# A two-layer MLP kernel: product 7 of matmul 2 in block 0 by an inner Strassen level

## The chip, the cores and the metric

The kernel runs on one core of a Trainium2 chip. The core has a matmul engine (TensorE, "PE" in the profile, with its weight loads shown as "PEld"), three elementwise engines (VectorE "DVE", ScalarE "ACT", GpSimd "POOL"), an engine that mainly issues transfers (SyncE "SP"), 16 DMA engines, a working memory of 128 partitions (SBUF) and eight accumulator banks of 512 fp32 values per partition (PSUM). Each engine runs its own instruction list in order; lists are tied together by semaphores. The metric is device time in microseconds; lower is better.

## The reference

```python
def reference(x, w1, b1, w2, b2):
    y = _layernorm(x, axis=-1)
    h = _gelu(jnp.einsum("bsd,df->bsf", y, w1) + b1)
    return jnp.einsum("bsf,fd->bsd", h, w2) + b2
```

x is 1 x 2048 x 1024, w1 is 1024 x 3584, w2 is 3584 x 1024, all in bf16. _layernorm subtracts the mean over the last axis and divides by the square root of the variance plus 1e-5; _gelu is the tanh approximation. The work is two matmuls of 2048 x 1024 x 3584 with a normalisation ahead, a gelu between and a bias at each.

## The kernel before, in words

**Blocks and products.** The 2048 tokens are two blocks of 1024 (s = 0 and 1). Within a block each of the two matmuls is done by Strassen's method in Winograd's form: operands are cut into quarters, seven products of quarters replace eight, and sums of quarters are formed before and after. For matmul 2 the left quarters are h[11], h[12], h[21], h[22] (512 tokens x 14 slices of 128 features), their sums S1 to S4, and the right quarters B11 to B22 of w2 with their sums T1 to T4. The order of products is SEQ2 = 1, 5, 2, 6, 7, 3, 4. Product 6 multiplies S2 by T2, product 7 multiplies S3 by T3. The sum of products 1 and 6 is called U here: it enters the output quarters 12 (with products 5 and 3), 21 (with 7 and 4) and 22 (with 7 and 5).

**Plain and inner products.** A product can be plain or inner. A plain one (plain, L974) is four groups, one per 128 tokens, of 14 matmuls with 512 columns each (L978). An inner one (inner, L1036) applies Strassen again: seven sub-products of 14 matmuls with 256 columns (sub, L1060, matmuls at L1063), after four sums of the left operand (tt, recorded at L854), and sums of the right one (inner_sums, L998: one large sum at L1022, or two where split is set, and two more at L854). inner_sums of block 0 also stores the sums to DRAM (keep), and block 1 loads them from there. An inner product's results leave PSUM in six VectorE adds and two ScalarE copies (k1, k5, k2, o11, o22, o12, o21, and a seed copy, all recorded at L942 and L962), each sub-product after the third waiting for an earlier one. INNER says which products are inner:

```python
INNER = ((1, 5, 2, 3, 4), SEQ2)
```

that is five of seven in block 0 and all of block 1. Since block 1 needs inner sums of T2 and T3 that block 0 does not make, t_inner (L1361) makes them during matmul 1 of block 1: it loads T2 or T3 to x_sb, forms three sums on VectorE (L1370) and stores them.

**Buffers.** yw_sb holds the normalised, transposed input during matmul 1 and pieces of w2 during matmul 2; w2a_sb holds two quarters of w2 (slots A and B); w1_sb, t1_sb, h_sb and o_sb are reused for sums once their first content is used up. sn_sb is 12 slots of fp32 rows for partial results. x_sb holds the eight input tiles of the next block, normalised by ScalarE (ln_act2, L464) during matmul 2 of block 0 and transposed into yw_sb by DMA (dma_T, L517). A tile of the second half has to wait with one of its transposes for the end of product 2, whose weights lie where it goes.

**Around the change.** In block 0 product 6 accumulates on U's banks hb, seeded with product 1's result. O12 (L1323) adds product 5 and keeps the result for output quarter 12. Product 7 then accumulates in the same four banks (L1329); four VectorE adds (L1336) make output quarter 22, and four ScalarE copies, O3 (L1340), keep the banks for product 4, which makes quarter 21.

**Order.** A planner (Planner.place, L149) places every operation when the kernel is built: it keeps a time for each engine, adds an estimated cost for each operation, and picks on the engine that is free first the one with the lowest due time among those that can start. ORDER adds a hand-made offset to the due time of some 170 operations by name. The outcome is a fixed list for each engine, with waits where an operation needs another engine's result or a freed buffer.

Of the kernel before, what the change touches and what calls it, by code (L numbers as in the profile page):

```python
# [32 lines left out]
INNER = ((1, 5, 2, 3, 4), SEQ2)  # L33
# [6 lines left out]
    G1_5g_0_5:5.5 G1_5g_1_5:8.8 G2_5g_0_3:-15.8 G2_5g_1_3:0.8 G3_5g_0_3:7.3 G3_5g_0_5:-4.7 G3_5g_1_1:-25.3  # L40
    G4_5g_1_1:13 G6_5g_0_5:-21 G7_5g_0_3:9.2 G7_5g_0_5:6.5 M11_1:8.3 M15_0:17 M24_0:-3.1 M27_1:5.7 M43_0:-8.5
    M47_0:7.7 M51_1:7.2 M57_0:16.8 M6_0_0:3.3 M72_1:-20.2 O12_0_1:11.2 O12_0_3:8.4 P1_0_6:10.3 P1_0_9:-1.1
    P1_1_2:-2.7 P1_1_3:-18.7 P1_1_6:0.2 P2_0_12:-1 P2_0_5:0.7 P3_0_10:-9.9 P3_0_11:5.1 P3_0_12:-7.3 P3_0_2:-10.3
    P3_1_6:9.8 P4_0_3:7.4 P4_0_9:-17.7 P4_1_0:40.5 P4_1_1:54.4 P4_1_3:2 P6_0_12:-3.6 P6_0_4:1.1 P6_1_11:4.1
    P7_0_6:-33.7 c7_0_11:2.3 c7_0_5:1.2 c7_0_8:-5.5 c7_0_9:8.4 c7_1_12:9.1 c7_1_13:1.2 g12_1_1:13.1 g12_1_3:2.2
    g21_1_8:25.8 g22_0_2:1.3 g22_0_3:1.6 gS0_5g_1_3:20 gS1_5g_0_3:-6.6 gS1_5g_0_5:11.2 gS3_5g_0_5:14.9 g_0_3_2:-14.6
    hS2_0_1:-7.5 hS3_1_0:8.3 hS4_0_1:-4.8 hS4_0_3:39 iS3_1_1_0:41 iS3_2_0_0:8.3 iS5_3_1_0:28.6 iS5_4_0_0:-14.1
    iS5_5_0_0:-10 iS6_5_0_0:-3.7 iT4_1_0_0:4.1 iT4_2_0_0:3.8 iT4_3_0_0:13.3 iT5_3_0_0:14.2 iT6_1_0_0:4.6
    iT6_2_0_0:1.3 iT6_4_0_0:6.6 iT6_5_0_0:-8.9 k5_3_1:16.7 k5_5g_0_5:35.6 o12_3_0:-17 pT1_2:-34.8 pT1_3:15 pT1_6:4.8
    pT2_1:1.7 pT2_2:7.7 pT3_3:10.8 pT3_5:-2.2 pT4_0:-7.2 pT4_3:-4.3 pT4_4:-7 pT4_5:-2.4 pT4_6:7.9 plain_0_7_2None:35  # L50
    plain_0_7_3None:8.5 pw2_0:-4.4 r11_5g_1_5:-18.2 r12_5_0:10.8 r22_1_0:14.3 r22_5g_0_3:33.7 s2_2_0:-7.2
    sd1_0_2:11.5 sn1_0_9:12.1 sn1_1_10:2.8 sn1_1_5:-0.5 sn5_0_4:-29.1 st0_5_0:-3.9 w1T13_1_0:3.4 w1T1_0_4:30.1
    w1T1_0_6:-5.1 w1T1_1_2:3.5 w1T2_1_1:26.1 w1T3_0_6:-17.7 w1T4_1_3:15 w1_0_0_1:9.9 w1_0_3_0:-7.9 w1_0_5_0:-24
    w1_0_5_1:-0.6 w1_1_0_0:0.7 w1_1_6_1:-1.9 w6_0_11:-4.1 w6_0_5:-9.5 w6_1_5:-44.2 wi5_3:20.8 x0_0_1:-11.2 x1_0:4.8
    y1_6:-8.5 yS1_1_0:6.2 yS2_0_0:8.2 yS2_1_0:-3.4 yS4_1_0:8.6 yi13_1:14.5 yi2_0:-15 yt0_6_0:-2.3
# [5 lines left out]
LAT = 0.12  # L61
PE_LAT = 0.2
# [43 lines left out]
class Planner:  # L106
# [42 lines left out]
    def place(self):  # L149
# [12 lines left out]
        while left:  # L162
# [35 lines left out]
            free[e] = r + c  # L198
# [60 lines left out]
def bass_standalone__mixer_channel_mlp__prompt_kernel(  # L259
# [24 lines left out]
    with ExitStack() as es:  # L284
# [584 lines left out]
        x_gate = {}  # L869
        PU = 2  # L870
# [58 lines left out]
        def mm2_block(s, W):  # L929
# [10 lines left out]
            last_ = {}  # L940
            done = lambda p: users[p]
# [10 lines left out]
            def bank_q(h_):  # L952
                return ps[:, h_.k, :].rearrange("p (v c) -> p v c", v=2)
# [82 lines left out]
            def inner(p, a, Yo, xb, war, O=None, bias=None, out=None, gate=(), ogate=(), kk=None, tmp=None, tail=False):  # L1036
# [21 lines left out]
                subs, ev = {}, {}  # L1058

# [68 lines left out]
                k1 = copy(kk_q, lambda: bank_q(c0), (subs[1], *gate), end(1), f"k1_{nm}", alloc=hk or tmp)  # L1128
# [55 lines left out]
            def last_block():  # L1184
# [82 lines left out]
                give(hold[7], sub7)  # L1267
                for i in range(2):
                    ho = Holder(outs, 2)
                    q = 10 * i + 11  # L1270
                    rows = lambda g, i=i: sn_sb[:, g.k + 2 * i:g.k + 2 * i + 2, :].rearrange(
                        "p j (v c) -> p v j c", v=2)
                    f = [add("DVE", 1.22, lambda e, i=i, ho=ho, rows=rows: plus(
                        e, o_sb[:, ho.k:ho.k + 2, :].rearrange("p v (j c) -> p v j c", j=2), rows(gw), rows(g5)),
                        (okq[q], okq[q + 1], *O12.values()), pt[7] + 7 * SUB + 0.1 * i, f"o22_{s}_{i}", alloc=ho,
                        frees=(g5,) if i else ())]
                    store(22, 2 * i, 2, ho, f, pt[7] + 7 * SUB)
# [5 lines left out]
            def war_of(subs, p=None):  # L1283
                return {(c, r): [subs[r]] + ([ti_st[p][r]] if c == "T" and r in ti_st.get(p, {}) else [])
                        for c in "ST" for r in subs}
# [41 lines left out]
            B[4] = load_w2(s, "H", "T4", done(6) + flat(S3, S4), pt[1] + 0.1, late=3.0)  # L1327

            M7 = plain(7, S3, B[7], hb, False, [(o,) for o in O12])  # L1329
            w1_use[n - 2] = w1_use[n - 2] + [M7[1]]  # L1330
            g3 = Holder(snaps, 4)
            O3 = []
            for t in range(TH):
                ho = Holder(outs)
                at = pt[7] + (t + 1) * SLOT2
                f = dve(lambda e, t=t, ho=ho: plus(e, o_sb[:, ho.k, :].rearrange("p (j c) -> p j c", j=2), bank_t(hb[t]),  # L1336
                                                   tile_of(g5, t)), (M7[t], *ok_t[t // 2]), at, f"o22_{s}_{t}", alloc=ho,
                        frees=(g5,) if t == TH - 1 else ())
                store(22, t, 1, ho, (f,), at)
                O3.append(copy(lambda t=t: tile_of(g3, t), lambda t=t: bank_t(hb[t]), (f, *O3[:1]), at + 0.7, f"O3_{s}_{t}",  # L1340
                               alloc=g3 if t == 0 else None, frees=(hb[t],)))

            sub3 = inner(3, S4, inner_sums(3, B[3], Y0, war_of(sub2, 2), True), X0, war_of(sub2), O=(g12, {11: O12[1], 12: O12[1], 21: O12[3], 22: O12[3]}), out=12)
            for m in (n - 1, n):
                w1_use[m] = w1_use[m] + done(3) + kept[3]
            for m in (n - 1, n):
                for k in range(1, 5):
# [5 lines left out]
                  halves(h_flat[21]), war4, O=(g3, {11: O3[1], 12: O3[1], 21: O3[3], 22: O3[3]}), out=21)  # L1353
# [3 lines left out]
            return {"A": done(3), "B": done(4) + kept[4], "C": done(2), "ring": ring, "p5": done(5), "p2": done(2), "outs": stores}  # L1357
# [49 lines left out]
        for s in range(NSB):  # L1407
# [27 lines left out]
            if s == 0:  # L1435
                W = {5: t1q, 1: t11, "C": last}
            else:
                x_end = [o for i in range(NT) for o in x_free[(s, i)]] + wfree["outs"]
                e6 = t_inner(6, 1, x_end + w1_use[NC], base1[s] + 0.2 * T_MM1)
                e7 = t_inner(7, 2, e6 + w1_use[NC + 2], base1[s] + 0.45 * T_MM1)  # L1440
                W = {"A": wfree["A"], "B": wfree["B"], "x": e7, "C": last}
            wfree = wf = mm2_block(s, W)
            if s + 1 < NSB:
                for c in range(N_W1):
                    load_w1(s + 1, c, base2[s] + 40 + c)
                for i in range(NT):
                    if i not in LN_EARLY:
                        load_x(s + 1, i, [*x_gate[i]], base2[s] - 4 + i)
                        k = (0, 1, 2, 2, 3, 4)[i]
                        ln_act2(s + 1, i, base2[s] + 6 + 8 * k,  # L1450
                                wf["ring"] + ([], [], wf["p5"], wf["p5"], wf["p2"])[k])
                    dma_T(s + 1, i, base2[s] + 20 + 6.3 * i, ((*last, *(wf["C"] if i >= TH else ())), last))
                y_sums(s + 1, base1[s + 1] - 4, wf["C"])
# [59 lines left out]
```

## Time and profile before

| | us |
|---|---|
| median of 9 runs (lowest, highest) | 338.63 (338.17, 340.62) |
| the profiled execution, its own time | 338.17 |
| its span, first to last instruction | 336.4 |
| TensorE busy in the span | 329.5 |
| VectorE busy | 281.7 |
| ScalarE busy | 173.4 |
| GpSimd busy | 22.3 |

The profile is that of one execution. Its span leaves out what lies around the instructions, so it is shorter than the execution's own time. L12 means line 12 of the kernel; where several operations go through one helper they share its line, so that L942 is any VectorE add made by dve, L962 any ScalarE copy made by copy and L854 any sum made by sums. A row of a group gives the output and inputs, partitions x elements and type, the count, the busy time, the mean duration in nanoseconds and the idle time of that engine just before. Consecutive instructions of one engine can overlap by a little at their ends. Block 0's matmul 1 ends and its matmul 2 begins near 95 us of the span; matmul 1 of block 1 begins near 172, its matmul 2 near 257.

### The profile page before, as it was taken

The page shows a single profiled execution, that of the slowest core. Times are in us where ns is not written, and L with a number is a line of the kernel's source. Part 1 is how long each engine was busy: PE and PEld are TensorE (multiplying, and loading weights), DVE is VectorE, ACT ScalarE, POOL GpSimd, SP SyncE. Part 2 cuts the span into 40 slices and gives each one's busy share as a digit, 9 for nine tenths or more (in the row PEclk, how much of TensorE's full clock was granted, in tenths as well). Part 3 has the DMA queues.
Part 4 walks back from the last instruction along what each step waited for, and adds up shares of the span by engine and source line. Part 5 has one row for each costly group of instructions (what it writes and reads, how often), then busy time and mean ns, then how long its engine had stood idle before and what let it go on. Part 6 is the DMA issues. An engine that isn't in the chain of part 4 may idle for free.

```text
span 336.4 us, 6035 instructions
## 1 busy us (share of the span) xinstructions
PE 329.5 (98%) x2399; PEld 223.5 (66%) x2399; DVE 281.7 (84%) x381; ACT 173.4 (52%) x292; POOL 22.3 (7%) x47
## 2 busy tenths in 40 slices
PE   4999999999999999999999999999999999999996
PEld 4977445455468885547875555544545888888885
DVE  3996789998999999979999878886738879999984
ACT  5775978566786687612113666765676521010200
POOL 2320120000020413200000000000000000000000
PEclk9899999999999999999999999999999999999999
DMA  7796999797869999899859549739971999998103
GB/s 237 265 205 185 356 348 323 245 330 257 286 238 301 364 355 337 223 308 384 323 171 331 172 181 337 286 136 287 350 233 54 383 314 361 338 364 278 64 0 127
DMA packets 80310, 89.47 MB, mean 266 GB/s; under 512 B 15130, under 2 KB 67226, under 8 KB 79770
## 3 DMA queue, kind: packets, MB, share of 16 engines
q1 hardware_dynamic: 80138, 88.95, 81.4%
q8 instruction: 19, 0.31, 0.4%
q10 hardware_dynamic: 144, 0.13, 0.1%
q14 instruction: 9, 0.07, 0.1%
HBM read 61.81 MB, written 24.38 MB: 256 GB/s over the span
## 4 chain that ended last, share of the span: by engine, by line
PE 93%; ACT 3%; POOL 1%; DVE 1%; DMA 1%; issue 0%
PE ps L767 42%; PE ps L1063 34%; PE ps L978 7%; PE ps L619 5%; PE ps L692 5%; DMA x_sb<-in_x_dram 1%; POOL st_sb L488 1%; PE ps L504 1%; ACT t_sb L474 1%; ACT t_sb L469 1%; PE ps L1068 0%; ACT sn_sb L962 0%; ACT ps L962 0%; DVE st_sb L418 0%; ACT x_sb L491 0%
## 5 line engine op out<-in xcount | busy, mean ns | idle before, releaser
L767 PE MATMUL ps<-yw_sb,t_sb 128*128 128x512 f16 x336 | 80.0, 379 | 0.0
L767 PE MATMUL ps<-yw_sb,w_sb 128*128 128x512 f16 x312 | 74.7, 379 | 0.0
L792 ACT ACTIVATE h_sb<-ps,b_sb 128x512 f16<-128x512 f32 x78 | 52.9, 687 | 37.0 <-PE ps L767 32.3
L767 PEld LDWEIGHTS ps<-yw_sb,t_sb 128*128 128x128 f16 x336 | 32.8, 98 | 35.9 <-DVE ps L807 0.6
L767 PEld LDWEIGHTS ps<-yw_sb,w_sb 128*128 128x128 bf16 x312 | 30.3, 98 | 33.1 <-ACT ps L780 0.3
L854 DVE TENSOR_TENSOR h_sb<-h_sb 128x2048 f16<-128x2048 f16 (+2 forms) x36 | 38.6, 1085 | 7.3 <-ACT h_sb L792 5.3
L962 ACT COPY sn_sb<-ps 128x512 f32<-128x512 f32 x27 | 15.5, 583 | 32.9 <-DVE o_sb L942 18.2
L1063 PE MATMUL ps<-w2a_sb,h_sb 128*128 128x256 f16 (+1 forms) x252 | 30.3, 273 | 0.0
L942 DVE TENSOR_TENSOR sn_sb<-ps,sn_sb 128x512 f32<-128x512 f32 x35 | 24.0, 688 | 5.3 <-PE ps L1063 4.5
L1063 PEld LDWEIGHTS ps<-w2a_sb,h_sb 128*128 128x128 f16 x252 | 24.7, 98 | 3.9
L942 DVE TENSOR_TENSOR o_sb<-ps,sn_sb 128x512 bf16<-128x512 f32 (+1 forms) x29 | 19.3, 670 | 6.3 <-PE ps L1063 3.7
L978 PE MATMUL ps<-w2a_sb,h_sb 128*128 128x512 f16 x112 | 24.5, 379 | 0.0
L1063 PE MATMUL ps<-w_sb,t_sb 128*128 128x256 f16 x196 | 23.4, 273 | 0.1
L962 ACT COPY ps<-sn_sb 128x512 f32<-128x512 f32 x12 | 7.1, 589 | 30.3 <-PE ps L1063 24.6
L780 ACT COPY ps<-ps 128x512 f32<-128x512 f32 x26 | 14.9, 577 | 14.5 <-PE ps L767 14.5
L587 DVE TENSOR_TENSOR t_sb<-w_sb,t_sb 128x1024 f16<-128x1024 bf16 x26 | 17.9, 688 | 3.6 <-DMA w_sb<-in_w_dram 2.4
L1063 PEld LDWEIGHTS ps<-w_sb,t_sb 128*128 128x128 f16 x196 | 19.0, 98 | 2.7 <-ACT sn_sb L962 0.4
L792 ACT ACTIVATE h_sb<-sn_sb,b_sb 128x512 f16<-128x512 f32 x26 | 18.5, 716 | 3.8 <-DVE sn_sb L821 2.9
L807 DVE TENSOR_TENSOR ps<-ps,sn_sb 128x512 f32<-128x512 f32 x26 | 17.6, 694 | 3.3 <-PE ps L767 3.1
L978 PEld LDWEIGHTS ps<-w2a_sb,h_sb 128*128 128x128 f16 x112 | 10.9, 98 | 12.8
L821 DVE TENSOR_TENSOR sn_sb<-ps,sn_sb 128x512 f32<-128x512 f32 x20 | 13.6, 687 | 4.5 <-PE ps L767 4.4
L619 PE MATMUL ps<-yw_sb,w_sb 128*128 128x128 f16 x256 | 16.9, 227 | 0.4 <-DVE yw_sb L511 0.4
(125 smaller groups left out, 485.6 us busy)
## 6 DMA issues: line engine op xcount, KB each, us to landing
w_sb<-in_w_dram SPq DMA_DIRECT2D x28, 512.0 KB, 5.8
x_sb<-in_w_dram SPq DMA_DIRECT2D x21, 256.0 KB, 6.0
w_sums<-x_sb SPq DMA_DIRECT2D x21, 256.0 KB, 3.8
w2a_sb<-w_inner_sums SPq DMA_DIRECT2D x12, 448.0 KB, 7.3
x_sb<-in_x_dram SPq DMA_DIRECT2D x15, 256.0 KB, 6.1
w_inner_sums<-w_sb SPq DMA_DIRECT2D x4, 896.0 KB, 8.3
x_sb<-w_sums SPq DMA_DIRECT2D x2, 1792.0 KB, 9.1
w_sb<-w_inner_sums SPq DMA_DIRECT2D x8, 448.0 KB, 7.0
```

The lines of the kernel that those rows point to most:

```text
L587: return add("DVE", 0.65, lambda e: e.tensor_tensor(out=tv(k), in0=x0, in1=x1, op=ALU.subtract), [*deps, *war.get(k, ())], prio + 0.5 * k, ...
L619: fn = [(lambda e, b=b, hb=hold[f], f=f, k=k, t=t: e.matmul(ps[:, hb.k, t * P:(t + 1) * P], lhsT=lhs[:, k, f * P:(f + 1) * P], rhs=yop[f"A ...
L692: fn = [(lambda e, k=k, v=v: e.matmul(ps[:, bank[r].k, v * QN:(v + 1) * QN], lhsT=xo()[:, k, v * P:(v + 1) * P], rhs=yv()[:, k, :], start= ...
L767: fn = [(lambda e, k=k: e.matmul(ps[:, hold[p].k, :], lhsT=lhs[:, k, :], rhs=yop[yo][:, k, :], start=(first and k == 0), stop=(k == KH - 1 ...
L780: return e.copy(out=dst, in_=src) if o_.eng == "ACT" else e.tensor_copy(dst, src)
L792: r = h_ok[(s, q, u)] = add("ACT", 0.70, lambda e: e.activation(out=dst, in_=src(), func=ACT.Gelu_apprx_tanh, bias=b1_sb[:, f:f + 1], scal ...
L807: o2 = add("DVE", 0.7, lambda e: e.tensor_tensor(out=b5v(b5), in0=b5v(b0), in1=v5(), op=ALU.add), (P6, *o5), pt[7] - SLOT, f"w6_{nm}", all ...
L854: o = add("DVE", cost2(w * dst.shape[-1]), lambda e, k0=k0, k1=k1: e.tensor_tensor(out=dst[:, k0:k1, :], in0=a[0][:, k0:k1, :], in1=b[0][: ...
L942: plus = lambda e, out, x, y: e.tensor_tensor(out=out, in0=x, in1=y, op=ALU.add)
L962: return act(lambda e: e.copy(out=out(), in_=src()), deps, at - 5, name, **k)
L978: fn = [(lambda e, k=k, t=t: e.matmul(ps[:, banks_[t].k, :], lhsT=a[0][:, k, t * P:(t + 1) * P], rhs=b[0][:, k, :], start=(first and k == ...
L1063: fn = [(lambda e, k=k, j=j: e.matmul(ps[:, bank[r].k, j * HI:(j + 1) * HI], lhsT=x[0][:, k, j * P:(j + 1) * P], rhs=y[0][:, k, :], start= ...
```

## The change

Product 7 of matmul 2 in block 0 becomes an inner product. Its weights' sums are formed in block 0 and stored; t_inner is no longer called for product 7. U is copied from the banks to gu by four ScalarE copies ahead of it, each bank freed by O12, which now follows the copy. The inner product adds its results onto gu, and two VectorE adds of twice the size make output quarter 22 from gu and product 5. Product 4 adds onto gu as well. The place for k1, product 7's first copy, is row 4 of x_sb, and so that copy waits until tile 4 of block 1 has been transposed (x_late); later loads into x_sb wait for k1's readers (x_users). Product 3's sums now wait for product 7's sub-products and stores, where they waited for product 2's. The planner takes 0.08 us off each VectorE and 0.09 us off each ScalarE operation for the overlap with the next, and ORDER has new entries throughout.

```diff
-INNER = ((1, 5, 2, 3, 4), SEQ2)
+INNER = ((1, 5, 2, 7, 3, 4), SEQ2)
 ...
+OVL = {"DVE": 0.08, "ACT": 0.09}
 ...
-            free[e] = r + c
+            free[e] = r + c - OVL.get(e, 0.0)
 ...
+        x_late = []
 ...
+                s_read[id(subs)] = {5: s2[1][0], 6: s4[1][0]}
 ...
-                k1 = copy(kk_q, lambda: bank_q(c0), (subs[1], *gate), end(1), f"k1_{nm}", alloc=hk or tmp)
+                first_k[p] = k1 = copy(kk_q, lambda: bank_q(c0), (subs[1], *gate), end(1), f"k1_{nm}", alloc=hk or tmp)
 ...
-
-            M7 = plain(7, S3, B[7], hb, False, [(o,) for o in O12])
-            w1_use[n - 2] = w1_use[n - 2] + [M7[1]]
-            g3 = Holder(snaps, 4)
-            O3 = []
+            gu = Holder(snaps, 4)
+            U = []
             for t in range(TH):
-                ho = Holder(outs)
-                at = pt[7] + (t + 1) * SLOT2
-                f = dve(lambda e, t=t, ho=ho: plus(e, o_sb[:, ho.k, :].rearrange("p (j c) -> p j c", j=2), bank_t(hb[t]),
-                                                   tile_of(g5, t)), (M7[t], *ok_t[t // 2]), at, f"o22_{s}_{t}", alloc=ho,
-                        frees=(g5,) if t == TH - 1 else ())
-                store(22, t, 1, ho, (f,), at)
-                O3.append(copy(lambda t=t: tile_of(g3, t), lambda t=t: bank_t(hb[t]), (f, *O3[:1]), at + 0.7, f"O3_{s}_{t}",
-                               alloc=g3 if t == 0 else None, frees=(hb[t],)))
-
-            sub3 = inner(3, S4, inner_sums(3, B[3], Y0, war_of(sub2, 2), True), X0, war_of(sub2), O=(g12, {11: O12[1], 12: O12[1], 21: O12[3], 22: O12[3]}), out=12)
+                U.append(copy(lambda t=t: tile_of(gu, t), lambda t=t: bank_t(hb[t]), (M6[t], *U[-1:]),
+                              pt[6] + (t + 1) * SLOT2, f"U_{s}_{t}", alloc=gu if t == 0 else None))
+                O12[t].frees = (hb[t],)
+                O12[t].deps.append(U[-1])
+
+            gw, okq, sub7 = inner(7, S3, inner_sums(7, B[7], Y0, war_of(sub2, 2)), X0, war_of(sub2),
+                                  O=(gu, {11: U[1], 12: U[1], 21: U[3], 22: U[3]}), kk=x_sb[:, TH, :].bitcast(F32))
+            x_late.append((first_k[7], (TH,)))
+            w1_use[n - 2] = w1_use[n - 2] + [sub7[5]]
+            f = []
+            for i in range(2):
+                ho = Holder(outs, 2)
+                q = 10 * i + 11
+                rows = lambda g, i=i: sn_sb[:, g.k + 2 * i:g.k + 2 * i + 2, :].rearrange("p j (v c) -> p v j c", v=2)
+                f = [add("DVE", 1.22, lambda e, i=i, ho=ho, rows=rows: plus(
+                    e, o_sb[:, ho.k:ho.k + 2, :].rearrange("p v (j c) -> p v j c", j=2), rows(gw), rows(g5)),
+                    (okq[q], okq[q + 1], *O12, *f), pt[7] + 7 * SUB + 0.1 * i, f"o22_{s}_{i}", alloc=ho,
+                    frees=(g5,) if i else ())]
+                store(22, 2 * i, 2, ho, f, pt[7] + 7 * SUB)
+            x_users = [okq[11]]
+
+            sub3 = inner(3, S4, inner_sums(3, B[3], Y0, war_of(sub7, 7), True), X0, war_of(sub7), O=(g12, {11: O12[1], 12: O12[1], 21: O12[3], 22: O12[3]}), out=12)
 ...
             inner(4, A[22], inner_sums(4, B[4], [two(w2b), *halves(w2b)[2:]], war4),
-                  halves(h_flat[21]), war4, O=(g3, {11: O3[1], 12: O3[1], 21: O3[3], 22: O3[3]}), out=21)
+                  halves(h_flat[21]), war4, O=(gw, okq), out=21, gate=(f[-1],))
 ...
-            return {"A": done(3), "B": done(4) + kept[4], "C": done(2), "ring": ring, "p5": done(5), "p2": done(2), "outs": stores}
+            return {"A": done(3), "B": done(4) + kept[4], "C": done(2), "ring": ring, "p5": done(5), "p2": done(2), "outs": stores + x_users}
 ...
-                e6 = t_inner(6, 1, x_end + w1_use[NC], base1[s] + 0.2 * T_MM1)
-                e7 = t_inner(7, 2, e6 + w1_use[NC + 2], base1[s] + 0.45 * T_MM1)
-                W = {"A": wfree["A"], "B": wfree["B"], "x": e7, "C": last}
+                e6 = t_inner(6, 1, x_end + w1_use[NC], base1[s] + 0.25 * T_MM1)
+                W = {"A": wfree["A"], "B": wfree["B"], "x": e6, "C": last}
 ...
+                for o, tiles in x_late:
+                    o.deps += [d for i in tiles for d in x_free[(s + 1, i)]]
```

## The prediction, made before the result was known

> **What bounds the kernel now.** I read the page's first part, then the waits of TensorE, then TensorE's timeline across matmul 2 of block 0, then VectorE's.
>
> From the page, busy time of each engine:
>
> ```profile
> PE 329.5 (98%) x2399; PEld 223.5 (66%) x2399; DVE 281.7 (84%) x381; ACT 173.4 (52%) x292; POOL 22.3 (7%) x47
> ```
>
> All that TensorE waited for (total us, times, longest):
>
> ```profile
> PE ps L504 <- DVE x_sb L429: 2.8, 1, 2.8
> PE ps L400 <- POOL ones L375: 1.0, 1, 1.0
> PE ps L619 <- DVE yw_sb L511: 0.4, 1, 0.4
> ```
>
> All three lie in the head. From then on TensorE is never seen waiting, so the end is set by the sum of its matmuls. Any matmul time removed is gained, provided nothing makes it wait.
>
> TensorE's timeline around product 7 (start, us):
>
> ```profile
> 126.71 6.21 PE L978 MATMUL ps<-w2a_sb,h_sb 128*128 128x512 f16 x28
> 132.75 1.69 PE L1063 MATMUL ps<-w_sb,h_sb 128*128 128x256 f16 x14
> 134.28 1.69 PE L1063 MATMUL ps<-yw_sb,t_sb 128*128 128x256 bf16 x14
> 135.81 18.29 PE L978 MATMUL ps<-w2a_sb,h_sb 128*128 128x512 f16 x84
> 153.94 1.69 PE L1063 MATMUL ps<-w2a_sb,h_sb 128*128 128x256 bf16 x14
> 155.47 1.69 PE L1063 MATMUL ps<-w_sb,t_sb 128*128 128x256 f16 x14
> ```
>
> A 512-column matmul costs (132.75 - 126.71) / 28 = 0.2157 us. An inner group of 14 with 256 columns costs 155.47 - 153.94 = 1.53 us, or 0.109 each. The 84 matmuls are the rest of product 6 (28) and all of product 7 (56), so product 7 starts near 141.9.
>
> The second engine to read is VectorE, by stretches (length, then PE, PEld, DVE, ACT, POOL busy; clock; DMA share; GB/s):
>
> ```profile
> 60.00:75.00 15.00, 15.00 (x75) 7.25 (x74) 14.65 (x25) 8.96 (x15) 0.00 (x0) 1.00 0.84 281
> 95.20:178.80 83.60, 83.48 (x630) 61.27 (x629) 77.33 (x87) 39.23 (x67) 11.91 (x18) 1.00 0.92 301
> 178.80:195.00 16.20, 16.20 (x89) 8.51 (x87) 13.68 (x24) 10.05 (x17) 0.00 (x0) 1.00 0.78 265
> ```
>
> From 95.2 to 178.8, the whole of matmul 2 in block 0, VectorE is busy 77.33 of 83.6 us. It is idle for 6.3, and DMA is busy for 92%. VectorE sets nothing yet, but it has hardly any room.
>
> **What the Trainium skill says.** "TensorE: Matmul & The Clock Gate", section Back-to-back issue gap, gives N/2.4 + 2.5 ns: 215.8 and 109.2 for 512 and 256 columns. The trace agrees (215.7, 109). "VectorE: DVE Perf Modes", section The perf-mode tier table, says that adding two tensors runs at one element a cycle when one is in PSUM, and at two for 16-bit SBUF data; the rows agree (512 f32 from PSUM 688 ns, 1792 f16 1085 ns). "Perfetto Trace Analysis", section Optimizing Scalar/DVE Operations, says that the write acknowledgement of one instruction overlaps the next. The trace agrees: adds of 0.68 us start 0.60 apart, 1.08 ones 1.00 apart, 1.22 ones 1.13 apart. I therefore count 0.08 less than the row's duration each. The same section advises giving work to ScalarE when VectorE is full, which the U copies do.
>
> **The change part by part.**
>
> TensorE: out go 56 x 0.2157 = 12.08 us. In come 7 groups x 14 x 0.109 = 98 x 0.109 = 10.68. Gain 1.40 us. The weight loads rise from 56 to 98, but run beside the matmuls in the inner groups already.
>
> VectorE in block 0. Removed: four adds into the output, 4 x 0.60 = 2.4. Added, all by periods: the sums of T3's quarters 1.93 + 1.0 + 1.0 = 3.9; the four sums of S3's quarters 4 x 1.0 = 4.0; six evictions of the inner product 6 x 0.60 = 3.6; two final adds over 1024 fp32 elements, 2 x 1.14 = 2.3, from this row of block 1:
>
> ```profile
> L942 DVE TENSOR_TENSOR o_sb<-sn_sb 128x1024 bf16<-128x1024 f32 x2 | 2.5, 1225 | 0.1
> ```
>
> Net +11.4 us between about 127 and 165. In block 1 the preparation of product 7's weights disappears (three sums at 222.7 to 226.9, 3.9 us, one load of 1792 KB and three stores of as much), but TensorE didn't wait for them, so they pay nothing. Those stores now leave in block 0.
>
> ScalarE: U's four copies replace those of product 7's result (0.58 us each). The inner product adds two. Its 39.2 busy of 83.6 us hide them; uncovered they would be 1.2 us.
>
> SyncE: three stores of sums come in, two of four output stores go, and the transposes and loads behind them slip by about half a microsecond of issue each.
>
> Now the fit. TensorE would reach the end of block 0 1.4 us earlier with 11.4 us more VectorE work before it, so VectorE must find 12.8 us by the first matmuls of block 1 that need its sums (t_sb at 178.79). It can find:
> - its idle time, 6.3, and 0.08 at each of some 12 gaps that would close, 1.0: together 7.3. Not all: the fullest stretch shown, 60 to 75, reaches 98%, so 2% of 83.6 = 1.7 stays idle. 5.6.
> - work done ahead of need. These lines lie before 178.79:
>
> ```profile
> 169.57 1.22 DVE L543 TENSOR_TENSOR yw_sb<-yw_sb 128x2048 f16<-128x2048 f16 x1
> 171.56 1.22 DVE L543 TENSOR_TENSOR yw_sb<-yw_sb 128x2048 f16<-128x2048 f16 x1
> 173.89 1.22 DVE L543 TENSOR_TENSOR yw_sb<-yw_sb 128x2048 f16<-128x2048 f16 x1
> 177.59 1.42 DVE L587 TENSOR_TENSOR t_sb<-w_sb,t_sb 128x1024 f16<-128x1024 bf16 x2
> ```
>
> Two of the y sums (2.3), the two weight sums (1.2) and one output add (0.6) can come later: 4.1. Then 178.8 to 195, now 84% busy, has to carry them.
> - matmuls of block 1 that need no sum. Those of two units already lie at 172 to 177. One more of 0.86 us may find a bank and its weights.
>
> Together 10.6, leaving 2.2 us that TensorE waits.
>
> Tile 4 and DMA: the copy k1 of product 7 goes into x_sb's row 4 and waits for both transposes of that tile. One of them can't start before product 2 ends at 135.8, and the last now leave late:
>
> ```profile
> 143.56 3.68 SPq L520 DMA_TRANSPOSE yw_sb<-x_sb  x2
> ```
>
> k1 must start by 144.2 (two groups into product 7, less its own 0.6). A transpose lands a median 5.3 us after issue, so 135.8 + 1.5 + 5.3 = 142.6 is in time if it goes first. Behind k1 on ScalarE stand the seed of the next product and normalisation of tile 5; product 7's third group waits for k1. B22, issued at 142.3, also meets 1.8 MB more stores, some 6 us at 300 GB/s, with product 3's second sum needing it by about 152. Bound for both: nothing (covered by product 6 and by 3 us between B22's landing and use) to 3 us. I take 0.6, as queues are 92% full.
>
> The remade table and the planner's overlap of 0.08/0.09 move other instructions. The gain can't exceed TensorE's total idle, 336.4 - 329.5 = 6.9, nearly all head and tail; the loss is open. I take 0, bounds -0.3 and +2.
>
> Sum: -1.4 + 2.2 + 0.6 = +1.4. The profiled execution took 338.17 us, 1.8 around its span of 336.4, so its successor would take about 339.6; the median of the runs is 0.5 higher, 338.63, giving **340.0 us**.
>
> **Rivals.**
> - All is hidden: idle time is used to the end (7.3), early work moves (4.1), two to three free matmul groups fill in (1.7 to 2.6). That is at least 13.1 against 12.8, so TensorE keeps its 1.4 us: 337.2. For: no waits now, ScalarE half idle, early transposes movable. Against: 84 us without one gap on an in-order engine. It decides if VectorE's share in this stretch passes 99%.
> - Even: part of the idle time gained, TensorE waits 0.4 to 2.4 us: about 338.6. For: the lower bound and my estimate stand only 2 us apart.
> - A transfer becomes the bound: tile 4's transpose or B22 arrives 3 us late on top of VectorE's 2.2: -1.4 + 2.2 + 3 = +3.8, 342.4. For: DMA share above 1.0 in the stretches from 145 to 160. Against: SyncE's order was written anew.
> - The change does not do what it says: the inner groups might run slower than 1.53 us. Products 2 and 3 show the same form at that rate; I give it nothing.
>
> **Numbers.** Chances: VectorE short, 339.65 to 341.5, 0.33; all hidden 0.25; even 0.30; transfer 0.12. Faster and slower begin at 0.3%, 1.0 us, about what a measurement of this kernel can tell from no change: 0.25 faster, 0.30 same, 0.45 slower. The likeliest case's own range is 339.6 to 341.5. The range of all, 337.0 to 342.6, takes in the hidden case and the transfer's centre.
>
> **What would show it.** Right: 98 L1063 matmuls in place of 56 L978 ones, the groups 1.53 us apart; VectorE 97% or more busy from 127 to 180; TensorE waiting for VectorE's sums or evictions in products 7, 3, 4 and the first unit of block 1, 2 to 3 us in all; the L543 sums later than 172. Wrong: no TensorE waits there (then 337.2), gaps on VectorE while TensorE waits for DMA or for k1 (then the transfer), or new waits far from block 0's matmul 2, which would be the table's.

## The result and the profile after

The changed kernel takes 342.77 us (median of 10 runs, 341.38 to 344.96) where the kernel before takes 338.73 in the same measurement (32 runs, 337.87 to 340.62): the ratio is 1.0123, 95% interval 1.0106 to 1.0140. It is slower by 4.0 us. The profiled execution took 342.23 us, its span 340.5, so it too stands 4.06 above that of before. (A correction to the description above: the table ORDER of the kernel before has 134 entries, not some 170.)

Busy time of each engine, from the page of the changed kernel:

```profile
PE 330.4 (97%) x2441; PEld 227.5 (67%) x2441; DVE 286.0 (84%) x389; ACT 173.8 (51%) x294; POOL 27.0 (8%) x47
```

There are 42 more matmuls, as there should be. GpSimd has the same 47 instructions, yet they take 4.7 us longer; nothing in the change gives GpSimd other work, and this is the first hint.

What TensorE waited for (total us, times, longest; the three rows left out lie in the head):

```profile
PE ps L1070 <- ACT ps L968: 1.8, 1, 1.8
...
PE ps L1070 <- DVE sn_sb L948: 0.9, 2, 0.6
...
PE ps L770 <- DVE t_sb L590: 0.4, 1, 0.4
PE ps L1070 <- DVE w_sb L857: 0.2, 1, 0.2
```

Before, nothing stood here outside the head. The longest of the new waits is not for VectorE but for a copy of ScalarE. TensorE's timeline through product 7 shows where it is:

```profile
142.65 1.69 PE L1070 MATMUL ps<-w2a_sb,h_sb 128*128 128x256 f16 x14
144.18 1.69 PE L1070 MATMUL ps<-w_sb,t_sb 128*128 128x256 f16 x14
147.68 1.70 PE L1070 MATMUL ps<-w2a_sb,h_sb 128*128 128x256 f16 x14 [1.81 <-ACT ps L968]
149.21 1.69 PE L1070 MATMUL ps<-w_sb,t_sb 128*128 128x256 f16 x14
151.17 1.70 PE L1070 MATMUL ps<-w2a_sb,t_sb 128*128 128x256 f16 x14 [0.26 <-DVE sn_sb L948]
153.50 1.70 PE L1070 MATMUL ps<-w_sb,t_sb 128*128 128x256 f16 x14 [0.63 <-DVE sn_sb L948]
```

Two groups start 1.53 us apart, as predicted; the third comes 3.50 after the second. Below I count a gap as the distance from one matmul's start to the next, less 0.2157 us for 512 columns or 0.109 for 256. Counted so, the first gap is 1.97 us, where the profile's own count of idle time is 1.81. In the profile of the changed kernel the gaps between 127 and 185 us are 1.97, 0.43, 0.79 and 0.13 in product 7, 0.40 at 170.8, and 0.17 and 0.57 at 182.6 and 183.6: together 4.46. Before, they are 0.0.

ScalarE's timeline at the same place:

```profile
134.07 1.24 ACT L494 ACTIVATE x_sb<-x_sb,st_sb,rstd_sb 128x1024 f16<-128x1024 bf16 x1 [3.68 <-POOL st_sb L491]
...
143.51 1.24 ACT L494 ACTIVATE x_sb<-x_sb,st_sb,rstd_sb 128x1024 f16<-128x1024 bf16 x1 [1.84 <-POOL st_sb L491]
144.66 2.47 ACT L968 COPY sn_sb<-ps 128x512 f32<-128x512 f32 x4
147.02 0.60 ACT L968 COPY ps<-sn_sb 128x512 f32<-128x512 f32 x1
147.54 0.59 ACT L968 COPY x_sb<-ps 128x512 f32<-128x512 f32 x1
```

L494 is the normalisation of a tile of block 1 (its result is called y): first tile 2's, then tile 5's. Behind tile 5's y stand the four copies of U, the seed and k1. TensorE had finished product 6 at 142.65, so U's last bank was ready when ScalarE still waited for GpSimd: the copies came 2 us late, and with them the seed (the copy ps<-sn_sb at 147.02), for which the third group of product 7 waits.

The kernel before has the same y, and there too it waited for GpSimd:

```profile
140.98 1.24 ACT L491 ACTIVATE x_sb<-x_sb,st_sb,rstd_sb 128x1024 f16<-128x1024 bf16 x1 [2.18 <-POOL st_sb L488]
```

It ended at 142.22, 0.4 us after product 6 (141.85), and the first copy behind it started at 145.80, when VectorE's add had released it. In the changed kernel it ended at 144.75, 2.1 us after product 6, with U's copies behind it. The wait was thus there to be seen ahead of the change; that it would end later was not.

VectorE shows the same wait from its side. Its first line is three of hS3's sums in one row (S3, the left operand of product 7); the last two are two of O12's four adds, which need U's copies:

```profile
131.04 2.95 DVE L857 TENSOR_TENSOR h_sb<-h_sb 128x2048 f16<-128x2048 f16 x3
...
145.32 0.69 DVE L948 TENSOR_TENSOR sn_sb<-ps,sn_sb 128x512 f32<-128x512 f32 x1 [2.81 <-ACT sn_sb L968]
146.49 0.69 DVE L948 TENSOR_TENSOR sn_sb<-ps,sn_sb 128x512 f32<-128x512 f32 x1 [0.47 <-ACT sn_sb L968]
```

VectorE loses 3.28 us just ahead of the stretch in which it has no spare time: from 147 to 180 us it is busy 32.76 of 33.0. GpSimd's timeline says why ScalarE waited. Each tile has three instructions of 128x1 elements; the first two lines are the second and third for tile 2, the last is the third for tile 5:

```profile
129.28 1.65 POOL L488 TENSOR_TENSOR rstd_sb<-vpe_sb,nhalf 128x1 f32<-128x1 f32 x1
131.00 3.03 POOL L491 TENSOR_TENSOR st_sb<-mv_sb,rstd_sb 128x1 f32<-128x1 f32 x1
...
143.28 0.19 POOL L491 TENSOR_TENSOR st_sb<-mv_sb,rstd_sb 128x1 f32<-128x1 f32 x1
```

The same instruction takes 0.19 us and 3.03 us. The long one runs from 131.00 to 134.03, just as long as VectorE's sums from 131.04 to 133.99. Tile 2's three took 5.0 us together (129.00 to 134.03); in the kernel before they took 1.35 (128.61 to 129.96):

```profile
129.15 0.55 POOL L485 TENSOR_TENSOR rstd_sb<-vpe_sb,nhalf 128x1 f32<-128x1 f32 x1
129.77 0.19 POOL L488 TENSOR_TENSOR st_sb<-mv_sb,rstd_sb 128x1 f32<-128x1 f32 x1
```

Beside these two VectorE ran additions from PSUM. The tiles are normalised one after another, so part of tile 2's delay is still in tile 5's y. SyncE's list, too, stands behind that y. Its issues in the changed kernel:

```profile
140.33 5.64 SPq L523 DMA_TRANSPOSE yw_sb<-x_sb  x4
146.02 0.58 SPq L353 DMA_DIRECT2D w_inner_sums<-w_sb  x1
146.64 1.99 SPq L523 DMA_TRANSPOSE yw_sb<-x_sb  x1
148.68 1.43 SPq L353 DMA_DIRECT2D w2a_sb<-in_w_dram  x2
```

Tile 5's transposes wait for its y, and B22 (w2a_sb) is issued behind them at 148.68; before, it was issued at 142.33, ahead of the last two transposes.

The profile thus adds up: -1.40 (less matmul time) + 4.46 (gaps) + 0.88 (the head: the last of its 128-column matmuls starts at 31.66, before at 30.78) = 3.94 of the 4.06 us. The head's share need not be the change's work: that start moves by as much among kernels with the same head (last section).

### The profile page after: what moved, and what is told of

The parts are those of the page before. It is cut to its first block, busy times and chain, and to the rows that moved or that the text cites. A ratio compares the mean times of both kernels' runs of the same rounds, so it can differ in the third digit from the quotient of the medians.

```text
span 340.5 us, 6132 instructions
## 1 busy us (share of the span) xinstructions
PE 330.4 (97%) x2441; PEld 227.5 (67%) x2441; DVE 286.0 (84%) x389; ACT 173.8 (51%) x294; POOL 27.0 (8%) x47
## 5 line engine op out<-in xcount | busy, mean ns | idle before, releaser
L770 PE MATMUL ps<-yw_sb,w_sb 128*128 128x512 f16 x312 | 75.5, 379 | 0.0
L770 PEld LDWEIGHTS ps<-yw_sb,w_sb 128*128 128x128 bf16 x312 | 30.3, 98 | 31.7 <-ACT ps L783 0.6
L1070 PE MATMUL ps<-w2a_sb,h_sb 128*128 128x256 f16 (+1 forms) x280 | 33.5, 273 | 1.8 <-ACT ps L968 1.8
L948 DVE TENSOR_TENSOR sn_sb<-ps,sn_sb 128x512 f32<-128x512 f32 x40 | 27.1, 686 | 8.0 <-PE ps L1070 4.6
L1070 PEld LDWEIGHTS ps<-w2a_sb,h_sb 128*128 128x128 f16 x280 | 27.1, 98 | 6.1 <-ACT ps L968 2.1
L1070 PE MATMUL ps<-w_sb,t_sb 128*128 128x256 f16 x238 | 28.3, 273 | 0.7 <-DVE sn_sb L948 0.6
L1070 PEld LDWEIGHTS ps<-w_sb,t_sb 128*128 128x128 f16 x238 | 23.1, 98 | 4.5 <-DVE sn_sb L948 0.9
L948 DVE TENSOR_TENSOR o_sb<-ps,sn_sb 128x512 bf16<-128x512 f32 (+1 forms) x25 | 16.7, 667 | 5.3 <-PE ps L1070 3.2
L857 DVE TENSOR_TENSOR t_sb<-h_sb 128x1792 f16<-128x1792 f16 x16 | 17.4, 1086 | 1.6 <-ACT h_sb L795 0.8
L622 PEld LDWEIGHTS ps<-yw_sb,w_sb 128*128 128x128 bf16 x256 | 16.1, 104 | 2.0 <-DMA w_sb<-in_w_dram 1.3
L1070 PE MATMUL ps<-w_sb,h_sb 128*128 128x256 f16 (+1 forms) x126 | 15.2, 273 | 0.2 <-DVE w_sb L857 0.2
```

What stands on the lines that cost most here:

```text
L622: fn = [(lambda e, b=b, hb=hold[f], f=f, k=k, t=t: e.matmul(ps[:, hb.k, t * P:(t + 1) * P], lhsT=lhs[:, k, f * P:(f + 1) * P], rhs=yop[f"A ...
L770: fn = [(lambda e, k=k: e.matmul(ps[:, hold[p].k, :], lhsT=lhs[:, k, :], rhs=yop[yo][:, k, :], start=(first and k == 0), stop=(k == KH - 1 ...
L857: o = add("DVE", cost2(w * dst.shape[-1]), lambda e, k0=k0, k1=k1: e.tensor_tensor(out=dst[:, k0:k1, :], in0=a[0][:, k0:k1, :], in1=b[0][: ...
L948: plus = lambda e, out, x, y: e.tensor_tensor(out=out, in0=x, in1=y, op=ALU.add)
L1070: fn = [(lambda e, k=k, j=j: e.matmul(ps[:, bank[r].k, j * HI:(j + 1) * HI], lhsT=x[0][:, k, j * P:(j + 1) * P], rhs=y[0][:, k, :], start= ...
```

## The experiments

All start from the changed kernel. Most move entries in the finished lists, after the planner, with this helper, and change nothing else:

```diff
+        def move(e, names, ahead_of):
+            mv = [o for n in names for o in order[e] if o.name == n]
+            rest = [o for o in order[e] if o not in mv]
+            k = next(k for k, o in enumerate(rest) if o.name == ahead_of)
+            order[e] = rest[:k] + mv + rest[k:]
```

### e1_u_first: ScalarE's list alone

```diff
+        move("ACT", [f"U_0_{t}" for t in range(TH)], "y1_5")
```

> Edit: the changed kernel, with the four copies of U moved ahead of tile 5's last normalisation step in ScalarE's list; nothing else moves. Queue theory (U stands behind a step that waits for GpSimd, and this makes both TensorE's first gap and VectorE's idle time, which is then missing later): TensorE's gap of 1.97 us at 145.6 shrinks below 0.5, VectorE's idle time of 3.3 us ahead of O12 below 1, and 2 to 3.5 us come back, so 339.3 to 340.8. Shortage theory (VectorE has too much work and the sum of the gaps is fixed by it): the first gap goes, but the later ones grow by as much; less than 1 us comes back, 341.8 to 342.8.

345.53 us (342.65 to 347.26, 4 runs), 1.018 times before (1.0111 to 1.0249): above both forecasts. The gap behind U is gone, and one wait of the sort shown above has taken its place:

```profile
PE ps L1070 <- DMA w2a_sb<-in_w_dram: 3.5, 1, 3.5
```

That is B22, issued at 152.01 behind tile 5's transposes, needed at 154.8. So two queues, not one, stand behind tile 5's y, and the first delay had hidden the second. The median is not this edit's price alone: the profiled execution (347.26) also lost 2.24 us between 115 and 123 us (see e8_y_behind), and 1.5 us in a stretch at half the granted clock that begins 0.9 us after this wait (last section).

### e2_u_b22_first: both queues

```diff
+        move("ACT", [f"U_0_{t}" for t in range(TH)], "y1_5")
+        move("SP", ["is7_0", "w2_0_B22_0", "w2_0_B22_1"], "yt1_5_0")
```

> Edit: as e1_u_first, and in SyncE's list the first store of product 7's sums and the two loads of B22 move ahead of tile 5's two transposes, so that they don't wait for tile 5 either. Queue theory: B22 is asked for at about 143 instead of 148.7; if e1_u_first shows TensorE or VectorE waiting for B22 at product 3 (1 to 3 us near 152), that wait goes here and the time is 338.5 to 340; if it shows none, the time is that of e1_u_first within 0.5. Shortage theory: no change against e1_u_first.

340.87 us (13 runs), ratio 1.0066 (1.0037 to 1.0095): about half of the loss is back, less than the queue theory said. Neither U nor B22 shows a gap any more. Part of what is left is the next thing on SyncE behind the same transposes: block 1's first weights, issued at 152.05, make TensorE wait 0.9 at 158, and a store that a sum has to wait for leaves late.

### e5_lists: all that stood behind tile 5's transposes

```diff
+        move("ACT", [f"U_0_{t}" for t in range(TH)], "y1_5")
+        move("SP", ["is7_0", "w2_0_B22_0", "w2_0_B22_1", "is7_2", "w1_1_0_0", "w1_1_0_1"], "yt1_5_0")
```

> Edit: as e2_u_b22_first, and the second store of product 7's sums and the first two weight loads of block 1 also move ahead of tile 5's two transposes in SyncE's list. In the profile of e2_u_b22_first TensorE still waited 1.1 us at 158 to 160 for those weights, and VectorE 1.5 us at 155.8 for that store. Queue theory: both waits go, and of the gaps of 2.7 us between 127 and 185 under 1.2 are left; 338.2 to 339.8, within 0.5 of the kernel before. Shortage theory: VectorE, busy without a break from 157 on, keeps TensorE waiting elsewhere for as long; 340.3 to 341.3.

338.66 us (22 runs), ratio 1.0008 (0.9988 to 1.0027): ten moved entries give back the 4 us, as the queue theory said, and the kernel is where the kernel before is. TensorE's waits outside the head:

```profile
PE ps L1070 <- ACT sn_sb L968: 1.8, 3, 0.9
...
PE ps L770 <- DVE t_sb L590: 0.4, 1, 0.4
PE ps L1070 <- DVE w_sb L857: 0.4, 1, 0.4
```

The first row lies at 115 to 123 us (see e8_y_behind). Between 127 and 185 us the gaps are 1.53 in place of 4.46 (0.54, 0.17 and 0.57, and 0.25 in smaller ones), more than the 1.2 that the theory allowed; the two that are long enough for the profile to name a cause wait for VectorE.

### e3_tile5_no_wait: take away what they wait for

Tile 5's y uses tile 4's statistics, so it does not wait for its own, and tile 5 is not normalised by its own mean and variance. The lists are unchanged.

```diff
-                out=x16[:, i, :], in_=x_sb[:, i, :], func=ACT.Identity, scale=rstd_sb[:, i:i + 1],
-                bias=st_sb[:, i, 1:2]), (nb, rs), prio + (0.006 if war is not None else 6.0), f"y{s}_{i}")
+                out=x16[:, i, :], in_=x_sb[:, i, :], func=ACT.Identity, scale=rstd_sb[:, i - (i == 5):i - (i == 5) + 1],
+                bias=st_sb[:, i - (i == 5), 1:2]), (nb, rs), prio + (0.006 if war is not None else 6.0), f"y{s}_{i}")
...
+        by = {o.name: o for ops in order.values() for o in ops}
+        by["y1_5"].deps = [d for d in by["y1_5"].deps if d.name not in ("nb1_5", "rstd1_5")] + [by["sq1_5"], by["nb1_4"]]
```

> Edit: the changed kernel with all lists as they are, but tile 5's last normalisation step takes its scale and offset from tile 4's statistics, so it needs nothing of the GpSimd chain of tile 5 (which still runs). The normalisation of tile 5 is left wrong by that. Queue theory: the step starts at about 141.7 instead of 143.5, the copies of U and all behind them 1.8 us earlier; 1.5 to 3 us come back, 339.8 to 341.3. Shortage theory: at most 0.5 us, 342.2 to 342.8.

342.05 us (4 runs), ratio 1.0100 (1.0050 to 1.0151), between the two forecasts and not to be told from the changed kernel; the profiled execution took 340.29, of which the head, 1.4 us shorter than in the changed kernel, is a large part. U's copies start at 141.64 and the gap behind them falls from 1.97 to 0.16. But B22, issued at 146.95, now costs 0.90, and VectorE 0.42 and 0.79 in product 7 as before. Taking away the last wait of the chain is not enough: y itself still comes at 140.5, held by tiles 2 and 4, and the queues stand behind it.

### e4_less_dve and e6_lists_less_dve: is VectorE the bound?

The seven sums for product 7's operands are cut from 256 to 16 columns, 6.5 us less work for VectorE; the second kernel has the moved entries of e5_lists as well. The rest of these sums is left out.

```diff
+                cc = 16 if name[0] == "i" and name.endswith("_7_0") else dst.shape[-1]
...
-                    out=dst[:, k0:k1, :], in0=a[0][:, k0:k1, :], in1=b[0][:, k0:k1, :], op=op),
+                    out=dst[:, k0:k1, 0:cc], in0=a[0][:, k0:k1, 0:cc], in1=b[0][:, k0:k1, 0:cc], op=op),
...
+                    cc = 16 if nm == "7_0" else HI
...
```

> Edit: the changed kernel with all lists as they are, but product 7's seven operand sums cover 16 of 256 columns each, so that VectorE has about 6.5 us less to do between 132 and 152; the rest of those sums is left out, so product 7 multiplies old data. Shortage theory: all gaps from 145 to 185 that end with VectorE or ScalarE go, 3.5 to 4.5 us come back, 338.3 to 339.3. Queue theory: the later gaps go (2.5 us), but the copies of U still stand behind tile 5's step, so that a gap of 1 to 2 us stays at 145; 339.8 to 341.0.

> Edit: e5_lists with product 7's seven operand sums cut to 16 of 256 columns (the rest of them is left out, product 7 multiplies old data), about 6.5 us less for VectorE. What it gains on e5_lists is VectorE's own share. Queue theory: under 1 us. Shortage theory: 1.5 us or more.

With the lists as they are: 342.02 us (4 runs), ratio 1.0082 (1.0052 to 1.0112). VectorE now waits 6.3 us for U's copies instead of 2.8, and TensorE 2.1 for B22; 6.5 us of work taken off the fullest engine gain about one, less than either forecast. The cut also speeds GpSimd up, since these are sums beside its instructions: tile 5's three take 1.09 us (140.67 to 141.76) in place of 1.71, U's copies start at 142.94 and the gap behind them falls to 0.25. So this run alone does not part VectorE's work from the queue; the next one does. With the lists in order: 338.48 us (12 runs), ratio 1.0004 (0.9985 to 1.0023), no faster than e5_lists. TensorE's only wait between 95 and 186 us is then

```profile
PE ps L770 <- DVE t_sb L590: 0.4, 1, 0.4
```

so 0.8 of the 1.53 us of gaps in e5_lists came from the amount of VectorE's work, and 0.73 (0.17 + 0.57) stays although VectorE now has idle time at 141 to 155: from 160 to 180 it is still busy 19.86 of 20.0 us.

### e7_less_hs3: the cause of the first delay

The four sums hS3 are cut from 512 to 16 columns and the rest of them is left out; nothing of tile 2 or GpSimd is touched.

```diff
+                cc = 16 if name == "hS3_0" else dst.shape[-1]
...
```

> Edit: the changed kernel with all lists as they are, but the four sums of S3 cut to 16 of 512 columns (the rest is left out), which takes VectorE's back-to-back SBUF sums from 125 to 134 out of GpSimd's way. If VectorE's sums hold GpSimd up: its three instructions for tile 2, which took 5.0 us (129.0 to 134.0), take under 2.5, and ScalarE's list behind them moves ahead by 2 us or more. If GpSimd is slow by itself: 4.5 us or more as before.

One execution, with a stretch at half the granted clock from 155.40 on (last section), so that its 343.24 us can't be compared. GpSimd's third instruction for tile 2, and the three for tile 5:

```profile
130.13 0.19 POOL L491 TENSOR_TENSOR st_sb<-mv_sb,rstd_sb 128x1 f32<-128x1 f32 x1
...
137.50 0.73 POOL L485 TENSOR_SCALAR vpe_sb<-st_sb 128x1 f32<-128x1 f32 x1 [3.60 <-ACT t_sb L477]
138.31 1.27 POOL L488 TENSOR_TENSOR rstd_sb<-vpe_sb,nhalf 128x1 f32<-128x1 f32 x1
139.66 1.50 POOL L491 TENSOR_TENSOR st_sb<-mv_sb,rstd_sb 128x1 f32<-128x1 f32 x1
```

The instruction of 3.03 us takes 0.19 and tile 2's three 1.48 instead of 5.03: the delay follows VectorE's sums, in this one execution. Tile 5's three now fall under other sums (136.36 to 141.1 without a break) and take 3.66 us. U's copies start at 142.34, and their gap is gone; B22 costs 2.14.

### e8_y_behind: the second level of times

The times of e5_lists have two levels: 16 of 22 executions at 337.2 to 339.5 us, 6 at 340.7 to 343.4. Its profile is one of the latter, with 2.24 us of gaps at 115 to 123 us, where ScalarE's y of tile 0 waited like this:

```profile
113.87 1.24 ACT L494 ACTIVATE x_sb<-x_sb,st_sb,rstd_sb 128x1024 f16<-128x1024 bf16 x1 [2.44 <-POOL st_sb L491]
```

GpSimd's three took 3.9 us for tile 0 there and 2.0 in e6_lists_less_dve, whose profile has none of these gaps; the lists up to that point are the same. In the kernel before, tile 0's y waited for GpSimd as well (2.00 us, until 116.98), but the copies k5_5, k2_5 and s2_2 had run ahead of it (112.47 to 114.98), and TensorE did not wait. Added to the moves of e5_lists:

```diff
+        move("ACT", ["k5_5_0", "sum1_1", "r21_1_0", "nm1_1", "k2_5_0"], "y1_0")
+        move("ACT", ["k1_2_0", "s2_2_0"], "y1_1")
```

> The ten entries of the run before, and on ScalarE's list two more moves: five entries (k5_5, the sum and the mean of tile 1, r21_1, k2_5) ahead of tile 0's y, and k1_2 and s2_2 ahead of tile 1's y, so that no copy of an inner product stands behind a y whose statistics GpSimd is late with. My theory: the executions of the run before at 340.7 to 343.4 us are those in which GpSimd's instructions for tiles 0 and 1 took 3.9 and 2.8 us and the y's held up the copies (2.2 us of gaps at 115 to 123 us in its profile). Then those gaps are gone in every execution, the median is 338.0 (337.3 to 338.7) and nothing above 340.5 is left. Rival: the two levels have another cause (DMA, or the cold clock of the head); then the spread and the median stay as they were, 338.7 with a quarter of the executions above 340.7.

338.42 us (22 runs, 336.98 to 341.18), ratio 0.9995 (0.9976 to 1.0014). The profiled execution (338.66) has no gap between 95 and 127 us, but two executions of 22 are still above 340.5 where there were six. Six against two of 22 could be chance, and the median can't be told from that of e5_lists, so it is supported, not settled, that the y's make the second level. The gaps between 127 and 185 us are 1.39.

### e9_sums_order and e10_two_sums: can order alone remove VectorE's gaps?

Both start from e8_y_behind. The first:

```diff
+        move("DVE", ["iT4_3_0_0"], "iS6_4_0_0")
+        move("DVE", ["o21_3_0"], "o11_4_0")
```

> The kernel with both moves on ScalarE, and on VectorE's list the operand sum T4 of product 3 one place earlier (ahead of S6 of product 4) and the output quarter O21 of product 3 behind the operand sums of block 1's product 5. My theory: what is left of VectorE's shortage are single instructions in the wrong place, 0.5 us at 170 us (T4 of product 3) and 0.17 + 0.57 us at 181 to 183 us (T13 and T2 of block 1); both go to below 0.1 us and the median falls 1.0 us (0.6 to 1.3) below that of the run with ScalarE's moves alone, to about 337.2, 0.4 to 0.5% below the kernel before. Rival: VectorE is short of time there and not only badly ordered; then the gaps come back a few microseconds later at S6 of product 4 or at block 1's other sums, and the median stays within 0.3 us.

340.84 us (10 runs), ratio 1.0062 (1.0038 to 1.0086): slower, which neither forecast said. The gap at 167 us is gone, but the output quarter that was put back by nine instructions frees a PSUM bank, and TensorE waits 2.7 us at 177.4 for it:

```profile
PE ps L770 <- DVE o_sb L948: 2.6, 1, 2.6
```

Another 1.5 us went in a stretch at half the granted clock right behind this wait (last section).

The second kernel:

```diff
+        move("DVE", ["iS6_3_0_0"], "iT6_3_0_0")
+        move("DVE", ["iT4_3_0_0"], "iS6_4_0_0")
```

> The kernel with both moves on ScalarE and two single moves on VectorE: the operand sum S6 of product 3 ahead of T6 of the same product (which waited 0.59 us for a store to leave its buffer), and T4 of product 3 ahead of S6 of product 4. No release of a PSUM bank is moved, as the output quarter of the run before was. My theory: VectorE has no idle time left between 147 and 181 us, the gaps at 159 and 167 us (0.10 and 0.55) go, and the one at 181 us stays near 0.7 us, because VectorE is really short there: 0.74 + 0.55 that TensorE comes earlier, less the 0.59 of idle time. The median falls 0.65 us (0.3 to 0.9) to about 337.8, 0.2 to 0.3% below the kernel before. Rival: VectorE is not short, only badly ordered; then the gap at 181 us shrinks as well and the median is 337.2 or less; or the earlier T4 holds up S6 of product 4 and nothing is won, 338.4.

338.70 us (14 runs), ratio 1.0008 (0.9989 to 1.0026): no gain. The gaps at 159 and 167 us went, and 0.07, 0.15 and 0.55 came at 162 to 170, the last for product 4's T6, whose place did not change; those at 179 and 180 are still 0.17 and 0.57. Taking away one wait brings TensorE sooner to the next: in both orders tried without a long wait (e8_y_behind and this one) TensorE waits 1.4 to 1.5 us up to the first matmuls of block 1.

### e11_pool_costs: give the planner the real durations

```diff
-            vp = add("POOL", 0.2, lambda e: e.tensor_scalar(out=vpe_sb[:, i:i + 1], in0=st_sb[:, i, 0:1],
+            vp = add("POOL", 0.42, lambda e: e.tensor_scalar(out=vpe_sb[:, i:i + 1], in0=st_sb[:, i, 0:1],
...
-            rs = add("POOL", 0.6, lambda e: e.tensor_tensor(out=rstd_sb[:, i:i + 1], in0=vpe_sb[:, i:i + 1],
+            rs = add("POOL", 0.98, lambda e: e.tensor_tensor(out=rstd_sb[:, i:i + 1], in0=vpe_sb[:, i:i + 1],
...
-            nb = add("POOL", 0.3, lambda e: e.tensor_tensor(out=st_sb[:, i, 1:2], in0=mv_sb[:, i, 1:2],
+            nb = add("POOL", 1.01, lambda e: e.tensor_tensor(out=st_sb[:, i, 1:2], in0=mv_sb[:, i, 1:2],
```

> Nothing but three numbers: the planner's costs of GpSimd's three instructions per tile of block 1, 0.2, 0.6 and 0.3 us, are set to the means that the trace of the changed kernel shows, 0.42, 0.98 and 1.01. No entry is moved by hand; the table and its due times stay. The planner then puts three of the four copies of U ahead of tile 5's y on ScalarE, and both loads of B22 ahead of tile 5's transposes on SyncE. My theory: the loss is the planner's wrong idea of when tile 5's statistics are there, so the gap of 2 us behind U goes without a gap at B22 in its place, and at least half of the 4 us comes back: 340.3 us (338.5 to 341.5). Rival: the due times of the table fit the old costs, the new order costs as much elsewhere (block 1's weights now stand behind tile 5's transposes, and the lists before 127 us change as well), and the time stays at 342 to 344.

344.64 us (6 runs), ratio 1.0146 (1.0110 to 1.0181): the rival was right, and the time lies above even its range. U and B22 cost nothing in its profile, as expected, but the new lists wait elsewhere. TensorE's three longest new waits lie at 247 (the longer one of the first row), 132 and 70 us:

```profile
PE ps L695 <- DVE sn_sb L677: 1.4, 2, 1.2
PE ps L1070 <- DVE o_sb L948: 1.2, 1, 1.2
PE ps L770 <- DVE ps L810: 1.1, 1, 1.1
```

Better costs under a table of due times made for the old ones change the lists far from U as well.

## Why the prediction was wrong

It gave 340.0 us with a range to 342.6; 342.77 was measured. The direction it held most likely, slower, was right, and so was one of its two reasons, VectorE; the larger part of the loss came from a wait that its sum does not have.

- **TensorE, -1.40: right.** 98 matmuls in groups 1.53 us apart replace 56. The section of the Trainium skill that the prediction cites, "Back-to-back issue gap" in "TensorE: Matmul & The Clock Gate", gives its formula for an isolated matmul and puts a sustained stream of 512 columns at about 131 ns each. The stream here ran at 215.7, so the measurement decides.
- **ScalarE's copies, "Its 39.2 busy of 83.6 us hide them": this is the step that failed.** A share of busy time says that ScalarE has time, not when. The copies stand in an in-order list behind tile 5's y, which waits for GpSimd. The sum puts this wait at nothing. The price was 1.97 us at TensorE, and 3.28 us of VectorE's time; with the lists in order (e5_lists) 2.93 of the 4.46 us of gaps are gone. SyncE's list was misjudged in the same way: "half a microsecond of issue each" became 6.35 us for B22 (142.33 to 148.68). I had named k1 and the seed as being queued behind one another, but did not ask what U itself is queued behind. The upper cost I gave for uncovered copies, 1.2 us, was only the duration of the two that are added.
- **VectorE short by 2.2: the mechanism is right, the size was off.** In the changed kernel the gaps apart from U's sum to 2.49 us (0.43 + 0.79 + 0.13 + 0.40 + 0.17 + 0.57), which comes near 2.2 by luck: part of it follows from the 3.28 us lost to U. With the lists in order it is 1.53 (e5_lists) and 1.39 (e8_y_behind); of the 1.53, 0.8 goes with 6.5 us less work.
- **Tile 4 and B22, 0.6, bounds 0 to 3: right object, wrong cause.** k1 began at 147.54, straight behind the seed, so tile 4's transposes held nothing up. B22 did come late, and by more than I took: 0.90, 2.1 and 3.6 us of wait in e3_tile5_no_wait, e4_less_dve and e1_u_first. It was not the stores or full DMA queues, but SyncE's order behind tile 5's transposes: with B22 ahead of them (e2_u_b22_first) its wait is gone. In the changed kernel itself B22's wait is hidden by U's.
- **The remade table, 0, bounds -0.3 to +2: too narrow.** The ten places that e5_lists moves come out of the new plan, and they are worth about 4 us (ratio 1.0123 to 1.0008). I priced the new order by nothing but TensorE's total idle.
- **Rivals.** The case "even" (part of the idle time gained, 0.4 to 2.4 us of waits, 338.6) describes what the change gives once the lists are in order: -1.40 + 1.5, 338.4 to 338.7 measured. "All is hidden" did not come about in any order tried. With the lists in order VectorE is idle for only 0.8 to 1.1 of the 53 us from 127 to 180 (e5_lists, e8_y_behind, e10_two_sums), less than the 1.4 to 1.5 us of gaps, so a new order within this stretch can't close them all. Moving work out of it was tried once (e9_sums_order) and held up a PSUM bank; other such moves stay untested. The transfer rival's figure, 342.4, came near by luck: tile 4 was on time, and B22 was late for another reason.
- **What I said would show it.** Gaps on VectorE while TensorE waits "for DMA or for k1" were nearly it: the gap is on VectorE, 2.81 us, but the wait is for U. VectorE's 97% from 127 to 180 was 93% in the changed kernel, and from 180 to 200 98% (19.62 of 20.0): work was pushed out of the first stretch. With the lists in order the 97% is exceeded. The third figure behind the comma below is VectorE's busy time from 127 to 180, in the changed kernel and in e5_lists:

```profile
127.00:180.00 53.00, 50.07 (x384) 36.70 (x382) 49.41 (x57) 17.58 (x31) 8.76 (x9) 1.00 0.88 294
127.00:180.00 53.00, 52.62 (x410) 39.09 (x408) 52.24 (x60) 18.14 (x31) 8.76 (x9) 1.00 0.94 299
```

What is open: whether tiles 0 and 1 alone make the second level of times, and why the planner's order, which put B22 ahead of the transposes before, no longer does so: that depends on its whole state, and no run parts the new table from the planner's new overlap of 0.08 and 0.09 us.

No version here beats the kernel before. The lowest, e8_y_behind, stands at 0.9995 (0.9976 to 1.0014) of it, which agrees with a saved 1.40 us against 1.39 us of gaps.

## What to carry to other kernels

For every instruction that a change adds or moves, write down what stands ahead of it in its engine's list and what that waits for: an engine that works its list in order and is idle half of the time can still be late. When a wait is removed, look for the next behind the same instruction on every queue, SyncE's included: here two delays hid one another, and mending one alone gained nothing. Look at what runs beside a chain of tiny GpSimd instructions. Here ten entries moved by hand gave back what the new plan had lost, and a new plan with the measured GpSimd durations (e11_pool_costs) did not.

## What the runs showed of the hardware

GpSimd's instructions of one element per partition were counted in all thirteen profiles from 25 us on. Those that ran beside no VectorE sum with both inputs in SBUF all took 0.19 us (41 of L485's and L491's kind) or 0.55 (21 of L488's kind); VectorE was idle or added from PSUM beside them. Beside such sums they took up to 3.03. All 49 of the first kind that took over 0.9 us ended 0.04 to 0.06 us after the end of a sum: 35 waited out one sum, 7 two and 7 three. In the changed kernel that is 1.10 us with one sum (from 109.80) and 3.03 with three (from 131.00). The kernel before has one of 2.82 us with two, for tile 0 at 114.12, so this too was there to be seen ahead of the change. What decides between one and three is not shown.

The Trainium skill says so in kind: "GPSIMD Engine Reference", section Specifications, gives GpSimd's SBUF interfaces as shared with VectorE, with contention for instructions "with two SBUF inputs". The trace agrees, and e7_less_hs3 shows the size: 1.48 against 5.03 us for three instructions.

The granted clock fell to half for 3.41 us between the head and the end in three profiles: from 159.39 in e1_u_first, 155.40 in e7_less_hs3 and 180.54 in e9_sums_order. Each time this began 0.3 to 0.9 us after the end of TensorE's longest wait outside the head (3.63, 2.14 and 2.73 us), and the matmuls in it took 1.4 to 1.5 us more. The profiles whose longest wait there was 2.11 us (e4_less_dve) or less have no such stretch. That the wait brings it was not tested.

The head is not constant: the last of its 128-column matmuls starts between 30.22 and 31.66 us in the profiles of kernels with the same head, so a single profile can't be read to better than about a microsecond there.
